# Start of a decode kernel: order of the first loads, longer rows for one weight, and two scalars over the software queue

## The chip, the cores and the metric

One core of one Trainium2 chip runs the kernel. Times are device microseconds. Before the change the kernel took 670.45 us (median of 3 runs, 669.8 to 670.9). The *span* is the part of an execution that the profile covers.

## The reference, cut to what matters

```python
x = A_x                                    # (4, 1, 640)
xn = layernorm(x)
# attention: q = xn @ wq (640 x 4096), 32 heads of 128; scores with k_cache (4,32,4096,128),
# softmax, times v_cache (4,32,4096,128), @ wo (4096 x 640)
# gMLP: z = gelu(xn @ w_in) (640 x 1728); z1, z2 = halves; z2 = layernorm(z2)
#       g = w_sp * z2 + b_sp               # w_sp and b_sp are one bf16 number each, as S = 1
#       (z1 * g) @ w_out (864 x 640)
return x + attention(xn) + gmlp(xn)
```

Each number of the caches (268 MB) and of the weights (14 MB) is used once, so some 282 MB have to come from HBM.

## The kernel before

Five buffers of 128 x 16,384 bf16 (4 MB each) take turns. The first holds w_in and w_out, the next two hold wq, then k and v units of 4 MB follow. All of this goes through the hardware queue of the SyncE engine (queue 1). The two scalars and x go through the hardware queue of ScalarE (queue 10); the trace shows them issued there in another order than written, the scalars at 0.74 and 1.31 us and x behind them at 1.96. In the views, xnT is the normalised and transposed x, QZ the tile in which q is laid out for the scores, and k0 the first unit of k. A packet record is the trace's entry for one piece of work of one DMA engine: start, duration and bytes.

```python
wg = kv_tile("w_gmlp")
w_in = wg[:, 0:n_in].rearrange("p (c f) -> p c f", c=DC)
nc.sync.dma_start(out=w_in, in_=B_w_in.rearrange("(p c) f -> p c f", c=DC))     # 17,280 B rows
nf = (FC - 1) * P                                                               # 768
nc.sync.dma_start(out=w_out[:, 0:FC - 1, :], in_=B_w_out[0:nf, :].rearrange("(c p) n -> p c n", p=P))
nc.sync.dma_start(out=w_out[:FL, FC - 1, :], in_=B_w_out[nf:Fh, :])             # 96 rows
... # wq in two loads, rows of 24,576 and 16,384 B
nc.scalar.dma_start(out=x_bf, in_=x_flat)
nc.scalar.dma_start(out=sb_bf[:, 0:1], in_=B_w_sp.rearrange("a b -> (a b)").to_broadcast((P, 1)))
nc.scalar.dma_start(out=sb_bf[:, 1:2], in_=B_b_sp.to_broadcast((P, 1)))
... # constants, layernorm of x, xnT
... # gMLP: 70 matmuls with w_in, gelu, layernorm, uT
... # q: 160 matmuls with wq, shuffles into q3
... # 14 matmuls uT x w_out into proj; then the loop over 32 k units and 32 v units
```

The broadcast of a scalar to 128 partitions is 128 pieces of two bytes.

Of the kernel before, what the change touches and what calls it, by code (L numbers as in the profile page):

```python
# [11 lines left out]
F32 = mybir.dt.float32  # L12
BF16 = mybir.dt.bfloat16
# [3 lines left out]
def kernel(  # L17
# [19 lines left out]
    nc = tc.nc  # L37
    P = 128
    B, Sq, D = A_x.shape
    _, H, Sk, Dh = A_k_cache.shape  # L40
    assert Sq == 1 and B == 4 and Dh == P and D % P == 0
    DC = D // P
# [10 lines left out]
    F2 = B_w_in.shape[1]  # L53
    Fh = F2 // 2
    FC = (Fh + P - 1) // P
    FL = Fh - (FC - 1) * P
    NOUT = A_wo.shape[1]
# [6 lines left out]
    const = ctx.enter_context(tc.tile_pool(name="const", bufs=1))  # L64
# [14 lines left out]
    def misc_ps(shape, dtype):  # L79
        misc_ctr[0] += 1  # L80
        return ps_m.tile(shape, dtype, tag="misc", name=f"misc{misc_ctr[0]}")
# [3 lines left out]
    def kv_tile(name):  # L85
        return kvpool.tile([P, KV], BF16, tag="kv", name=name)
# [3 lines left out]
    out_flat = out.rearrange("b s d -> (b s) d")  # L90


    wg = kv_tile("w_gmlp")
    n_in = DC * F2
    w_in = wg[:, 0:n_in].rearrange("p (c f) -> p c f", c=DC)
    nc.sync.dma_start(out=w_in, in_=B_w_in.rearrange("(p c) f -> p c f", c=DC))
    w_out = wg[:, n_in:n_in + FC * NOUT].rearrange("p (c n) -> p c n", c=FC)
    nf = (FC - 1) * P
    nc.sync.dma_start(out=w_out[:, 0:FC - 1, :], in_=B_w_out[0:nf, :].rearrange("(c p) n -> p c n", p=P))
    nc.sync.dma_start(out=w_out[:FL, FC - 1, :], in_=B_w_out[nf:Fh, :])  # L100

    wq_v = A_wq.rearrange("(p c) n -> p c n", c=DC)
    wq_t = []
    for i, (c0, c1) in enumerate(((0, 3), (3, DC))):
        wt = kv_tile(f"wq{i}")
        n = (c1 - c0) * H * Dh
# [4 lines left out]
    x_bf = wt[:B, KV // 2 + 7 * D:KV // 2 + 8 * D]  # L111
    nc.scalar.dma_start(out=x_bf, in_=x_flat)
    sb_bf = const.tile([P, 2], BF16)
    nc.scalar.dma_start(out=sb_bf[:, 0:1], in_=B_w_sp.rearrange("a b -> (a b)").to_broadcast((P, 1)))
    nc.scalar.dma_start(out=sb_bf[:, 1:2], in_=B_b_sp.to_broadcast((P, 1)))
    sb_f = const.tile([P, 2], F32)


    ident_bf = const.tile([P, P], BF16)
# [28 lines left out]
    xnT = const.tile([P, DC, B], BF16)  # L148
# [23 lines left out]
    for bb in range(2):  # L172
        nc.vector.tensor_copy(out=SelG[:, bb, :, :, 2 * bb:2 * bb + 2],
                              in_=I32[:].rearrange("p (b h c) -> p c h b", b=2, c=NCH))
# [12 lines left out]
    Pm = const.tile([P, 4, HG, 32], BF16)  # L187
    for hd in range(HG):
        nc.vector.tensor_copy(out=Pm[:, :, hd, :].rearrange("p (a w) j -> p a w j", w=2),
                              in_=ident_bf[:].rearrange("p (a j w) -> p a w j", a=2, w=2))  # L190
# [9 lines left out]
    proj = ps_j.tile([64, 512], F32)  # L200


    zT_ps = ps_g.tile([P, 2, FC, B], F32)
    for part in range(2):
        for fc in range(FC):
            n = P if fc < FC - 1 else FL
            f0 = part * Fh + fc * P
            for c in range(DC):
                nc.tensor.matmul(zT_ps[:n, part, fc, :], lhsT=w_in[:, c, f0:f0 + n],  # L209
                                 rhs=xnT[:, c, :], start=(c == 0), stop=(c == DC - 1))  # L210
    zT = const.tile([P, 2, FC, B], F32)
    nc.vector.memset(zT[:], 0.0)
# [1 line left out]
    nc.vector.memset(uT[:], 0.0)  # L214
    nc.scalar.activation(out=zT[:, :, 0:FC - 1, :], in_=zT_ps[:, :, 0:FC - 1, :], func=ACT.Gelu_apprx_tanh)
    nc.scalar.activation(out=zT[:FL, :, FC - 1, :], in_=zT_ps[:FL, :, FC - 1, :], func=ACT.Gelu_apprx_tanh)
    nc.vector.tensor_copy(out=sb_f[:], in_=sb_bf[:])
    z1 = zT[:, 0, :, :]
    z2 = zT[:, 1, :, :]
    st_in = const.tile([P, 2, FC, B], F32)  # L220
# [4 lines left out]
                     rhs=st_in[:].rearrange("p s c b -> p (s c b)"), start=True, stop=True)  # L225
# [17 lines left out]
    nc.vector.tensor_scalar(out=t1[:], in0=t1[:], scalar1=sb_f[:, 0:1], scalar2=sb_f[:, 1:2],  # L243
                            op0=ALU.mult, op1=ALU.add)
    nc.vector.tensor_tensor(out=uT[:, :, 0:B], in0=z1, in1=t1[:], op=ALU.mult)


    q_ps = misc_ps([P, H, B], F32)
    for h in range(H):
        for c in range(DC):  # L250
            nc.tensor.matmul(q_ps[:, h, :], lhsT=wq_t[c][:, h * Dh:(h + 1) * Dh], rhs=xnT[:, c, :],  # L251
                             start=(c == 0), stop=(c == DC - 1))
    q_bf = const.tile([P, H * B], BF16)
    nc.vector.tensor_copy(out=q_bf[:], in_=q_ps[:].rearrange("p h b -> p (h b)"))
    q3_ps = misc_ps([P, 4, H * B], F32)
    for kw in range(4):
        nc.tensor.matmul(q3_ps[:, kw, :], lhsT=Pm[:, kw, :, :].rearrange("p a j -> p (a j)"), rhs=q_bf[:],
                         start=True, stop=True)
    q3 = const.tile([P, 4, H * B], BF16)
    nc.vector.tensor_copy(out=q3[:], in_=q3_ps[:])  # L260


    for fc in range(FC):
        n = P if fc < FC - 1 else FL
        nb = B if fc else 32
        for hf in range(NH):
            nc.tensor.matmul(proj[32 * hf:32 * hf + nb, 0:NO2], lhsT=uT[:n, fc, 0:nb],
                             rhs=w_out[:n, fc, hf * NO2:(hf + 1) * NO2], start=(fc == 0), stop=False)
# [221 lines left out]
    for s in range(NS):  # L490
# [19 lines left out]
        if 0 <= v < NU - 1:  # L510
            emit_V(v, vc)
            g, b = divmod(v, B)
# [8 lines left out]
        elif v == NU - 1 and vc == 0:  # L521
# [8 lines left out]
            for t in range(T):  # L530
                a, c, e = t // 64, t // 16 % 4, t % 16
# [40 lines left out]
```

## Time and profile before

| | before |
|---|---|
| span of the profiled run | 669.1 us |
| share of the DMA engines' time used by queue 1 | 98.6% |
| rate in the middle 609 us | 431 GB/s |
| first transpose of the first k unit (k0) starts | 37.91 us |
| PE, DVE busy | 50%, 48% |

The first transpose of k0, as the trace has it (37.91 is its start, 3.20 us the wait for k before it):

```profile
37.91 8.89 DVE L318 STREAM_TRANSPOSE kT<-k 128x2048 f32<-128x2048 f32 x4 [3.20 <-DMA k<-in_A_k_cache_dram]
```

The page's slices show the DMA rate in 40 slices of 16.7 us. All but the first and the last lie between 418 and 441 GB/s. A kernel like this can gain only at the ends of the stream or in its bytes, and the change is made to the first 30 us.

To measure that stretch I use a sum that the document calls **stream lost**. It takes the packet records of a trace, spreads the bytes of each over its duration, sets the first packet of queue 1 at 1.75 us, adds the bytes moved from 1.5 to 32.5 us, and counts by how many microseconds they fall short of 431 GB/s. For the kernel before it is 3.57 us. The lines of stretches count a packet where it starts, so a short stretch can differ there from this sum by some tens of GB/s.

### The profile page before, as it was taken

What the parts mean: (1) busy time and instruction counts of PE and PEld (TensorE: products, weight loads), DVE (VectorE), ACT (ScalarE), POOL (GpSimd) and SP (SyncE); (2) the same over time, 40 slices, a digit from 0 to 9 for tenths busy, and PEclk for the clock granted to TensorE, in tenths of its full rate; (3) what the DMA queues carried; (4) which work ended last, traced back from release to release, by engine and by line L of the source; (5) the groups of instructions that cost most, each with busy time, mean ns of one, the idle gap of its engine ahead of it and who ended that gap; (6) DMA issues with size and microseconds to landing.
All of it is one profiled execution on the core that took longest, in us unless ns stands there. A gap on an engine that the chain in (4) does not pass through costs nothing.

```text
span 669.1 us, 6401 instructions
## 1 busy us (share of the span) xinstructions
PE 335.7 (50%) x2781; PEld 139.1 (21%) x2781; DVE 319.5 (48%) x253; ACT 60.4 (9%) x184; POOL 8.9 (1%) x40
## 2 busy tenths in 40 slices
PE   0647463546543664337555364454753366433745
PEld 0511121122111221113121031111311122111323
DVE  4279853465533455542555534346543355543300
ACT  0200210012000210003000030001200021000300
POOL 0010000000000000000000000000000000000000
PEclk9997777778777787676766677866767878567676
DMA  8999999999999999999999999999999999999995
GB/s 313 439 424 428 436 433 428 425 436 431 426 435 430 428 434 439 424 428 434 427 429 433 432 427 434 426 427 441 428 431 430 431 427 432 433 433 426 435 418 230
DMA packets 12900, 282.65 MB, mean 422 GB/s; under 512 B 1621, under 2 KB 3017, under 8 KB 4169
## 3 DMA queue, kind: packets, MB, share of 16 engines
q1 hardware_dynamic: 12568, 282.25, 98.6%
q8 instruction: 21, 0.34, 0.2%
q10 hardware_dynamic: 304, 0.01, 0.0%
q14 instruction: 7, 0.05, 0.0%
HBM read 282.25 MB, written 0.01 MB: 422 GB/s over the span
## 4 chain that ended last, share of the span: by engine, by line
DMA 56%; PE 15%; issue 13%; DVE 12%; ACT 3%; ACTq 0%; DVEq 0%
DMA k<-in_A_k_cache_dram 50%; DVE kT L318 8%; PE O L422 6%; DMA wo_last<-in_A_wo_dram 5%; PE S L336 3%; ACT p L364 3%; PE misc L439 2%; DMA sb_bf<-in_B_b_sp_dram 2%; PE x L377 1%; DVE m L343 1%; DVE om L442 1%; PE misc L251 1%; PE misc L347 1%; ACT O_sb L430 0%; PE zT_ps L209 0%
## 5 line engine op out<-in xcount | busy, mean ns | idle before, releaser
L318 DVE STREAM_TRANSPOSE kT<-k 128x2048 f32<-128x2048 f32 x128 | 284.6, 2280 | 215.0 <-DMA k<-in_A_k_cache_dram 212.4
L336 PE MATMUL S<-kT,QZ 128*32 128x512 bf16 x1024 | 203.7, 538 | 257.6 <-DVE kT L318 255.2
L336 PEld LDWEIGHTS <-QZ 128*32 128x32 bf16 x1024 | 57.3, 115 | 399.1 <-issue 386.7
L422 PE MATMUL O<-v,Zb 128*32 128x512 bf16 x992 | 93.1, 467 | 9.0 <-DMA v<-in_A_v_cache_dram 9.0
L422 PEld LDWEIGHTS <-Zb 128*32 128x32 bf16 x992 | 42.1, 112 | 41.0 <-issue 26.2
L364 ACT ACTIVATE p<-S,negmax 128x1024 bf16<-128x1024 f32 x16 | 17.7, 1109 | 272.0 <-DVE negmax L358 272.0
L430 ACT COPY O_sb<-O 128x512 f32<-128x512 f32 x16 | 9.4, 585 | 240.6 <-PE O L422 240.6
L388 ACT COPY Zb<-x 32x128 bf16<-32x128 bf16 x128 | 27.3, 255 | 10.2 <-PE x L377 9.5
L377 PE MATMUL x<-IdP,p 128*128 128x128 bf16 x128 | 16.1, 305 | 18.9 <-ACT p L364 18.6
L442 DVE SCALAR_TENSOR_TENSOR om<-misc,rinv,MkH 16x512 bf16<-16x512 f32 x7 | 5.2, 739 | 37.8 <-PE misc L439 37.8
L439 PE MATMUL misc<-O_sb,SelG 128*16 128x128 f32 x112 | 16.9, 289 | 2.0 <-DVE rinv L398 1.5
L377 PEld LDWEIGHTS <-p 128*128 128x128 bf16 x128 | 12.0, 138 | 22.6 <-ACT p L364 22.6
L275 POOL COPY QZ<-q 32x16 bf16<-32x16 bf16 x32 | 7.9, 246 | 455.4 <-PE S L336 420.9
L439 PEld LDWEIGHTS misc<-O_sb,SelG 128*16 128x16 f32 x112 | 10.1, 99 | 7.9 <-ACT O_sb L430 2.4
L474 DVE TENSOR_TENSOR oL<-misc,rinv 128x8 bf16<-128x8 f32 (+1 forms) x2 | 0.3, 168 | 22.6 <-PE misc L472 22.6
L343 DVE TENSOR_REDUCE m<-S 128x1 f32<-128x512 f32 x8 | 5.5, 691 | 10.2 <-PE S L336 10.2
L147 PE MATMUL misc<-ident_bf,wq 4*128 4x4 bf16 x5 | 0.4, 178 | 18.9 <-DVE wq L143 18.9
L368 DVE TENSOR_TENSOR rowsum<-rs 128x1 f32<-128x1 f32 x8 | 1.2, 155 | 17.0 <-ACT p L364 17.0
L347 PE MATMUL misc<-dg,ones_f 128*128 128x128 f32 x16 | 3.9, 324 | 9.0 <-DVE dg L345 9.0
L364 ACT ACT_TABLE_LOAD x1 | 1.3, 1283 | 54.8 <-DVE negmax L358 54.8
L460 PE MATMUL proj<-wo,oT 128*4 128x320 bf16 x56 | 5.0, 298 | 1.9 <-DVE oT L453 1.9
L251 PE MATMUL misc<-xnT,wq 128*128 128x4 bf16 x160 | 4.7, 166 | 1.1 <-issue 0.8
(93 smaller groups left out, 75.9 us busy)
## 6 DMA issues: line engine op xcount, KB each, us to landing
k<-in_A_k_cache_dram SPq DMA_DIRECT2D x32, 4096.0 KB, 43.3
v<-in_A_v_cache_dram SPq DMA_DIRECT2D x31, 4096.0 KB, 41.1
wo<-in_A_wo_dram SPq DMA_DIRECT2D x7, 640.0 KB, 44.6
wq<-in_A_wq_dram SPq DMA_DIRECT2D x1, 3072.0 KB, 19.5
w_gmlp<-in_B_w_in_dram SPq DMA_DIRECT2D x1, 2160.0 KB, 9.3
wq<-in_A_wq_dram SPq DMA_DIRECT2D x1, 2048.0 KB
v<-in_A_v_cache_dram SPq DMA_DIRECT2D x1, 2048.0 KB
v<-in_A_v_cache_dram SPq DMA_DIRECT2D x1, 1024.0 KB, 38.4
```

The lines of the kernel that those rows point to most:

```text
L251: nc.tensor.matmul(q_ps[:, h, :], lhsT=wq_t[c][:, h * Dh:(h + 1) * Dh], rhs=xnT[:, c, :], start=(c == 0), stop=(c == DC - 1))
L318: nc.vector.transpose(kT[:], kw[:, ch * n:(ch + 1) * n])
L336: nc.tensor.matmul(S_ps[32 * q:32 * q + 32, :, :], lhsT=qz[:, b, kw, w0:w0 + 32], rhs=kT[:, i, :, kw // 2, :, kw % 2], start=(b == 0 and c ...
L343: nc.vector.tensor_reduce(out=m1[:], in_=S_ps[:].rearrange("p k m -> p (k m)"), axis=AX.X, op=ALU.max)
L347: nc.tensor.matmul(mm[:], lhsT=ones_f[:], rhs=dg[:], start=True, stop=True)
L364: nc.scalar.activation(out=p_i[:], in_=S_ps[:, 8 * i:8 * i + 8, None, :].to_broadcast((P, 8, HG, M)), func=ACT.Exp, bias=negmax[:, 0:1], s ...
L377: nc.tensor.transpose(x[:, t, :], p_bf[t // 8][:, t % 8].rearrange("p h m -> p (h m)"), IdP[:])
L388: nc.scalar.copy(out=dst, in_=src[:, 2 * bb + b1])
L422: nc.tensor.matmul(O_ps[32 * q:32 * q + 32, :, :], lhsT=Zb[bb][:, w0:w0 + 32], rhs=vv[:, e // 16, e % 16, :, :], start=(b1 == 0 and e < 4) ...
L430: nc.scalar.copy(out=O_sb[:], in_=O_ps[:])
L439: nc.tensor.matmul(oh[:], lhsT=SelG[:, bb, c].rearrange("p h b -> p (h b)"), rhs=O_sb[:, c, :], start=(bb == 0 and c == 0), stop=(bb == 1 ...
L442: nc.vector.scalar_tensor_tensor(out=om[:], in0=oh[:, None, :].to_broadcast((G, HG, Dh)), scalar=state.pop(("rinv", g))[:, 0:1], in1=MkH[: ...
```

## The change

The intent: load wq first and compute q first, so that what the attention needs is there early; give w_out long rows; take the scalars out of the way of x and of the hardware queues.

```diff
+    nc.sync.dma_start(wq ...)            # both halves first, then x on nc.scalar
-    nc.scalar.dma_start(out=sb_bf[:, 0:1], in_=B_w_sp...to_broadcast((P, 1)))
-    nc.scalar.dma_start(out=sb_bf[:, 1:2], in_=B_b_sp.to_broadcast((P, 1)))
+    nc.gpsimd.dma_start(out=sb_bf[:, 0:1], in_=B_w_sp...to_broadcast((P, 1)))
+    nc.gpsimd.dma_start(out=sb_bf[:, 1:2], in_=B_b_sp.to_broadcast((P, 1)))
...  # w_in, w_out now after wq
-    ... in_=B_w_out[0:nf, :].rearrange("(c p) n -> p c n", p=P))     # 768 rows of 1,280 B
+    ... in_=B_w_out[0:nf, :].rearrange("(p c) n -> p c n", p=P))     # 128 rows of 7,680 B
...  # q, q3 moved ahead of the gMLP
-                nc.tensor.matmul(..., lhsT=w_in[:, c, f0:f0 + n], ...)
+                    w = w_in[:, c, f0:f0 + nf].rearrange("p (f a) -> p a f", a=FC - 1)[:, fc, :]
+                nc.tensor.matmul(..., lhsT=w, ...)                   # every sixth column
-    nc.vector.tensor_copy(out=sb_f[:], in_=sb_bf[:])
+    nc.gpsimd.tensor_copy(out=sb_f[:], in_=sb_bf[:])
```

More of the change, by code (lines that the diff above doesn't have):

```diff
@@ L90 @@
     out_flat = out.rearrange("b s d -> (b s) d")
-    wg = kv_tile("w_gmlp")
-    n_in = DC * F2
-    w_in = wg[:, 0:n_in].rearrange("p (c f) -> p c f", c=DC)
-    nc.sync.dma_start(out=w_in, in_=B_w_in.rearrange("(p c) f -> p c f", c=DC))
-    w_out = wg[:, n_in:n_in + FC * NOUT].rearrange("p (c n) -> p c n", c=FC)
-    nf = (FC - 1) * P
-    nc.sync.dma_start(out=w_out[:, 0:FC - 1, :], in_=B_w_out[0:nf, :].rearrange("(c p) n -> p c n", p=P))
-    nc.sync.dma_start(out=w_out[:FL, FC - 1, :], in_=B_w_out[nf:Fh, :])
     wq_v = A_wq.rearrange("(p c) n -> p c n", c=DC)
@@ L113 @@
     sb_bf = const.tile([P, 2], BF16)
-    nc.scalar.dma_start(out=sb_bf[:, 0:1], in_=B_w_sp.rearrange("a b -> (a b)").to_broadcast((P, 1)))
-    nc.scalar.dma_start(out=sb_bf[:, 1:2], in_=B_b_sp.to_broadcast((P, 1)))
+    nc.gpsimd.dma_start(out=sb_bf[:, 0:1], in_=B_w_sp.rearrange("a b -> (a b)").to_broadcast((P, 1)))
+    nc.gpsimd.dma_start(out=sb_bf[:, 1:2], in_=B_b_sp.to_broadcast((P, 1)))
     sb_f = const.tile([P, 2], F32)
+    wg = kv_tile("w_gmlp")
+    n_in = DC * F2
+    w_in = wg[:, 0:n_in].rearrange("p (c f) -> p c f", c=DC)
+    nc.sync.dma_start(out=w_in, in_=B_w_in.rearrange("(p c) f -> p c f", c=DC))
+    w_out = wg[:, n_in:n_in + FC * NOUT].rearrange("p (c n) -> p c n", c=FC)
+    nf = (FC - 1) * P
+    nc.sync.dma_start(out=w_out[:, 0:FC - 1, :], in_=B_w_out[0:nf, :].rearrange("(p c) n -> p c n", p=P))
+    nc.sync.dma_start(out=w_out[:FL, FC - 1, :], in_=B_w_out[nf:Fh, :])
     ident_bf = const.tile([P, P], BF16)
@@ L200 @@
     proj = ps_j.tile([64, 512], F32)
+    q_ps = misc_ps([P, H, B], F32)
+    for h in range(H):
+        for c in range(DC):
+            nc.tensor.matmul(q_ps[:, h, :], lhsT=wq_t[c][:, h * Dh:(h + 1) * Dh], rhs=xnT[:, c, :],
+                             start=(c == 0), stop=(c == DC - 1))
+    q_bf = const.tile([P, H * B], BF16)
+    nc.vector.tensor_copy(out=q_bf[:], in_=q_ps[:].rearrange("p h b -> p (h b)"))
+    q3_ps = misc_ps([P, 4, H * B], F32)
+    for kw in range(4):
+        nc.tensor.matmul(q3_ps[:, kw, :], lhsT=Pm[:, kw, :, :].rearrange("p a j -> p (a j)"), rhs=q_bf[:],
+                         start=True, stop=True)
+    q3 = const.tile([P, 4, H * B], BF16)
+    nc.vector.tensor_copy(out=q3[:], in_=q3_ps[:])
     zT_ps = ps_g.tile([P, 2, FC, B], F32)
@@ L206 @@
             n = P if fc < FC - 1 else FL
-            f0 = part * Fh + fc * P
+            f0 = part * Fh
             for c in range(DC):
-                nc.tensor.matmul(zT_ps[:n, part, fc, :], lhsT=w_in[:, c, f0:f0 + n],
+                if fc < FC - 1:
+                    w = w_in[:, c, f0:f0 + nf].rearrange("p (f a) -> p a f", a=FC - 1)[:, fc, :]
+                else:
+                    w = w_in[:, c, f0 + nf:f0 + Fh]
+                nc.tensor.matmul(zT_ps[:n, part, fc, :], lhsT=w,
                                  rhs=xnT[:, c, :], start=(c == 0), stop=(c == DC - 1))
@@ L245 @@
     nc.vector.tensor_tensor(out=uT[:, :, 0:B], in0=z1, in1=t1[:], op=ALU.mult)
-    q_ps = misc_ps([P, H, B], F32)
-    for h in range(H):
-        for c in range(DC):
-            nc.tensor.matmul(q_ps[:, h, :], lhsT=wq_t[c][:, h * Dh:(h + 1) * Dh], rhs=xnT[:, c, :],
-                             start=(c == 0), stop=(c == DC - 1))
-    q_bf = const.tile([P, H * B], BF16)
-    nc.vector.tensor_copy(out=q_bf[:], in_=q_ps[:].rearrange("p h b -> p (h b)"))
-    q3_ps = misc_ps([P, 4, H * B], F32)
-    for kw in range(4):
-        nc.tensor.matmul(q3_ps[:, kw, :], lhsT=Pm[:, kw, :, :].rearrange("p a j -> p (a j)"), rhs=q_bf[:],
-                         start=True, stop=True)
-    q3 = const.tile([P, 4, H * B], BF16)
-    nc.vector.tensor_copy(out=q3[:], in_=q3_ps[:])
     for fc in range(FC):
```

## The prediction

> **What bounds the kernel now.** I read the page's queue table and slices first, because 282 MB for one core is a lot of traffic for 670 us.
>
> ```profile
> q1 hardware_dynamic: 12568, 282.25, 98.6%
> GB/s 313 439 424 428 436 433 428 425 436 431 426 435 430 428 434 439 424 428 434 427 429 433 432 427 434 426 427 441 428 431 430 431 427 432 433 433 426 435 418 230
> ...
> L318 DVE STREAM_TRANSPOSE kT<-k 128x2048 f32<-128x2048 f32 x128 | 284.6, 2280 | 215.0 <-DMA k<-in_A_k_cache_dram 212.4
> ...
> k<-in_A_k_cache_dram SPq DMA_DIRECT2D x32, 4096.0 KB, 43.3
> w_gmlp<-in_B_w_out_dram SPq DMA_DIRECT2D x1, 960.0 KB, 12.8
> ```
>
> One queue keeps the 16 DMA engines 98.6% busy. PE is busy 50% of the span and DVE 48%, and DVE's largest idle time, 212.4 us, is waiting for k to land. A k load lands a median 43.3 us after its issue. One 4 MB unit takes 4.194 MB / 431 GB/s = 9.7 us, so a load is issued with some 3.5 other units still ahead of it. A wait of an engine for a buffer, or of the issuing queue for a semaphore, therefore costs nothing unless it exceeds about 30 us. The chain of waits agrees: its largest item is the k loads, 50%.
>
> So the time is start-up, plus bytes over the rate, plus what the stream loses at its two ends, plus a short tail. I then cut the stream by stretches (columns: stretch, length, busy time of PE, PEld, DVE, ACT and POOL with counts, clock, DMA share, GB/s; a packet counts in the stretch in which it starts, so short stretches are rough):
>
> ```profile
> 0.00:5.00 5.00, 0.00 (x0) 0.00 (x0) 3.01 (x9) 1.28 (x1) 1.08 (x8) 1.00 0.66 218
> 5.00:8.00 3.00, 0.00 (x0) 0.00 (x0) 0.00 (x0) 0.00 (x0) 0.00 (x0) 1.00 0.97 363
> 8.00:11.00 3.00, 0.00 (x0) 0.00 (x0) 0.00 (x0) 0.00 (x0) 0.00 (x0) 1.00 0.68 216
> 11.00:15.00 4.00, 0.00 (x0) 0.00 (x0) 3.16 (x21) 0.00 (x0) 0.00 (x0) 1.00 1.12 413
> ...
> 25.00:634.00 609.00, 312.95 (x2431) 124.06 (x2431) 306.68 (x202) 53.08 (x169) 7.86 (x32) 0.74 1.00 431
> 634.00:660.00 26.00, 14.65 (x172) 8.35 (x171) 1.25 (x4) 2.57 (x9) 0.00 (x0) 0.74 0.98 414
> 660.00:669.00 9.00, 4.37 (x107) 3.23 (x103) 0.65 (x2) 0.00 (x0) 0.00 (x0) 0.51 0.24 87
> ```
>
> The middle 609 us run at 431 GB/s with all engines busy, and the change touches nothing there. The losses are in the first 15 us. From 0 to 5 us there is 1.76 us before the first packet and then a ramp (the first 17,280 B packets take 1.1 to 1.7 us each, later ones 0.644). From 5 to 15 us, 363x3 + 216x3 + 413x4 = 3,389 KB move where 4,310 could, so 921/431 = 2.1 us are lost. This is where w_out (row by row) and the two scalars are on the engines. The total loss available to the change is about this 2.1 us.
>
> The same 15 us hold the compute that the change reorders. The chain of waits begins there with the scalars:
>
> ```profile
> 1.31 10.32 DMA sb_bf<-in_B_b_sp_dram
> 13.57 0.53 DVE Pm L189 x4
> 14.11 0.41 DVE wq L130
> ...
> 25.72 2.05 PE proj L267 x14
> 27.78 3.53 PE misc L251 x129
> 31.31 0.79 issue
> 32.10 0.88 PE misc L251 x28
> 32.98 33.90 DMA k<-in_A_k_cache_dram
> ```
>
> DVE sits 7.5 us in its program order before the cast of the two scalars, and the layernorm of x (from 14.1) is behind it. The last line looks as though q, by releasing the wq buffers, sets when a k load starts. But that load lands 33.9 us after its issue because it queues behind others, so an earlier release only lengthens its queueing.
>
> **What the Trainium skill says.** "DMA: Bandwidth & Descriptors", section "Why small descriptors are slow (HBM only)", gives a fixed overhead per packet and per descriptor. The trace agrees in direction: 32,768 B packets take a median 1.215 us (27.0 GB/s per engine), 1,280 B packets 0.055 us median and 0.059 mean (21.6), 5,120 B packets 0.199 (25.8), 8,192 B packets 0.313 (26.1). The same page, section "Issuing engines are not separate DMA queues", says that DMAs from any issuing engine run on the same 16 engines and interleave. The trace shows it: the scalars' 2 B packets on queue 10 lie between the w_in and w_out packets of queue 1. Hence moving the scalars to the software queue should not remove their 256 packets. "SBUF — State Buffer", section on the port swizzle, note on SBUF cachelines, says consecutive reads that leave a 16 B line pay a penalty. The new w_in weight loads step 12 B between columns; no trace of before has such a load, its packed ones take 104 ns.
>
> **The change part by part.**
>
> 1. Order of the big loads: wq (5.24 MB) before w_in, w_out (3.32 MB). The sum before k0 is equal, so k0's position in the stream does not move. Alone worth 0.
>
> 2. w_out in rows of 7.5 KB: 768 packets of 1,280 B become 128 of 7,680 B. Transfer: 768 x 0.059 / 16 = 2.83 us before; 128 x 0.295 (estimate, 7,680 B at 26.0 GB/s from the rows above) / 16 = 2.36 us after; saves 0.5 us. On top, between 8 and 9.5 us the engines are about half idle in the packet records, 0.7 us of stream, just where w_in runs out and w_out starts, and w_out's packets do not yet flow. I think that the many small rows are not made fast enough, right at the front of the queue. After the change there are a sixth of the rows and 22 us of loads ahead of them, so I count most of this 0.7 as saved: 0.6. The last 96 rows of w_out stay at 1,280 B, a sixth of the packets of before, so some loss stays. Sum: 1.1 us.
>
> 3. Scalars on the software queue, x alone on the other: the 256 packets stay (9 ns each, 0.13 us per engine), but they come early, beside 24 KB packets. From 6.3 to 8 us the engines deliver 310 to 350 GB/s while 2 B packets alternate with 17,280 B ones; if that alternation is the cause, 0.3 to 0.4 us. I cannot tell whether it moves or goes. I count 0.2.
>
> 4. DVE no longer waits for the scalars, and x need not follow them. The layernorm can start at about 4.5 us (estimate, x issued at 0.7) in place of 14.1, and xnT be ready near 10 in place of 19.5. Then wq lands at about 1.8 + 5.24/0.431 + 1.5 ramp = 15.5 plus 1 for the last engine, against 26 before; q (160 matmuls, 4.7 us busy), the shuffles (2 us) and the QZ fill (2.4) end near 26 in place of 37.1. The gMLP waits for w_gmlp, near 24 to 25, and takes the 8.2 us that it took from 19.56 to 27.77, ending near 33; k0 lands near 36. All of it beside the stream: 0 us of the end. The strided weight loads, 60 of them, would cost 60 x 0.3 = 18 us even if four times as slow (estimate), and that too hides in the 30 us of queued loads.
>
> 5. The tail from 660 us on keeps its instructions and its order.
>
> Sum: 0 + 1.1 + 0.2 + 0 + 0 = 1.3 us. 670.45 - 1.3 = 669.15, say 669.2.
>
> **The rivals.**
>
> A. Nothing gained. Each load runs in 16 shares and the end is set by the slowest engine: in the records the engines finish between 659.5 and 664.5. If the engines that end last lost least in the first 15 us, the gain is eaten. Against: between 8 and 9.5 us the loss was on nearly all engines. It gives 670.2 to 670.8.
>
> B. The gain is up to the whole 2.1 us, and 0.3 of the ramp also goes since x and the scalars are out of the way: 668.2. For: 2 B packets and 1,280 B rows are everywhere in that stretch. Against: both remain in part.
>
> C. A new wait. The software queue's descriptors are made by GpSimd ahead of the identity matrices, which the transposes of x and IdP need; or the strided weight loads hold PE while k0 arrives, so that S starts late. For: in the new program order PE does the gMLP's last matmuls before the first S. Against: k0's buffer is not needed for a new load before the 30 us of queue are used up. A late start of even 15 us gives 0; only well above 30 us would the stream starve. It makes 671 to 680, chance 2%.
>
> D. The earlier q lets the whole pipeline start earlier, by the 11 us by which QZ is ready sooner: 660. The chain of waits suggests it. Against: the first transpose waits for k0, which lands at 37.9 whatever q does, and bytes over rate allow no such gain.
>
> **Range and chances.** The three runs of before spread over 1.1 us. The gain is 0 to 2.4. So 669.2, with 668.0 to 670.5 in 8 of 10. Two per cent is 13.4 us, and only a starved stream (C) or a gain that the bytes do not allow (D) gets there: faster 0.005, same 0.985, slower 0.01.
>
> **What would show it.** Right: the first slice of 16.7 us rises from 313 to about 340 GB/s, while the middle stays at 431; no dip to half where w_out runs; q ends near 26 us, gMLP near 33; the first transpose of k0 starts 1 to 1.5 us earlier than 37.9, and so does wo_last's landing. Step 2 is wrong if a dip of the same depth appears elsewhere; step 3 if the scalars' packets slow wq0; step 4 if S of k0 starts later than 40.3 and the loads near 75 us show gaps. The whole is wrong if the middle stretch leaves 431 GB/s.

## The result, and the profile after

The changed kernel took 670.16 us (median of 4 runs, 669.91 to 670.24) against 670.33 for the kernel before in the same measurement. The ratio is 0.9997, with a 95% interval of 0.9979 to 1.0014. Ratios here are the mean time of one kernel's fast runs over the mean of the other's of the same rounds, so not quite the ratio of the medians quoted. The time is the same, and inside the predicted range. The gain of 1.3 us did not show. The interval alone does not exclude it (1.3 us would be a ratio of 0.9981); that of the repeat further down does (0.9990 to 1.0021), and so does the stream lost.

The page of the changed kernel, its slices and its queues:

```profile
GB/s 329 429 420 429 437 437 421 429 441 420 431 437 421 436 434 433 422 434 434 423 434 434 427 433 432 429 430 435 429 432 431 430 431 433 428 434 429 430 425 243
...
q1 hardware_dynamic: 11928, 282.25, 98.7%
...
q0 software_dynamic: 64, 0.00, 0.0%
q10 hardware_dynamic: 16, 0.01, 0.0%
```

The first slice rose from 313 to 329 GB/s and not to 340; the rest is as before. Queue 1 has 640 packets fewer, which is w_out's 768 rows turned into 128. The scalars' 256 packets have gone from queue 10, and a queue 0 has come with 64.

The stretches of the changed kernel (columns as in the prediction):

```profile
0.00:5.00 5.00, 0.00 (x0) 0.00 (x0) 3.80 (x10) 1.28 (x1) 2.53 (x10) 1.00 0.70 232
5.00:8.00 3.00, 0.00 (x0) 0.00 (x0) 2.94 (x12) 0.48 (x2) 0.00 (x0) 1.00 0.49 205
8.00:11.00 3.00, 0.35 (x5) 0.27 (x5) 2.22 (x17) 1.09 (x1) 0.00 (x0) 1.00 1.06 451
11.00:15.00 4.00, 0.24 (x3) 0.16 (x3) 0.00 (x0) 0.00 (x0) 0.18 (x1) 1.00 0.94 403
...
25.00:634.00 609.00, 308.08 (x2316) 122.86 (x2315) 306.94 (x208) 55.97 (x178) 7.12 (x29) 0.74 1.00 430
634.00:660.00 26.00, 14.49 (x191) 8.39 (x190) 1.25 (x4) 1.57 (x4) 0.00 (x0) 0.72 0.98 414
```

The weak stretch from 8 to 11 us has gone (216 to 451 GB/s), and the stretch from 5 to 8 us has fallen from 363 to 205, with the engines busy for half of it. In the packet records the rate between 6.0 and 8.0 us is 240, 56, 68 and 106 GB/s in its half microseconds. This hole costs 1.6 us of stream. It lies in the first wq load, whose packets are of 24,576 B, and the first records of queue 0 follow at 6.6 us.

The compute of the start behaved about as predicted. From the changed kernel's order of time:

```profile
9.61 0.35 PE L148 MATMUL misc<-ident_bf,wq 4*128 4x4 bf16 x5 [9.61 <-DVE wq L144]
...
17.91 4.34 PE L207 MATMUL misc<-xnT,wq 128*128 128x4 bf16 x157 [4.66 <-DMA wq<-in_A_wq_dram]
...
24.02 2.42 POOL L280 COPY QZ<-q 32x16 bf16<-32x16 bf16 x8 [11.65 <-DVE q L216]
...
30.55 2.05 PE L272 MATMUL proj<-w_gmlp,uT 128*32 128x320 bf16 x14 [2.30 <-DVE uT L265]
...
36.59 8.89 DVE L323 STREAM_TRANSPOSE kT<-k 128x2048 f32<-128x2048 f32 x4 [6.10 <-DMA k<-in_A_k_cache_dram]
```

The columns are start, time from start to end, engine, line, operation, and in brackets the idle time before and what ended it. The transposes of x start at 9.6 us instead of 18.9, QZ is full at 26.4 instead of 37.1, the gMLP ends at 32.6, and the first transpose of k0 waits 6.1 us for its load. All of this is early, and the time shows none of it.

That first transpose starts 1.3 us earlier than before, and the span is 0.9 us shorter. So two of the prediction's signs of being right, an earlier k0 and an earlier wo_last (its matmuls start at 663.89 instead of 664.95), did appear. But that profiled pair flatters the change. In the 9 timed runs of the kernel before in the first batch below, the spans alternate between 667.9 to 668.0 and 668.8 to 669.1, and its profile is one of the long ones. The first four spans of the changed kernel are 667.9 to 668.2. Why the spans have two levels is open. Other kernels show the upper one too, and k0's first transpose can carry it: e5 below was profiled at 668.9 us and has it at 37.39, with no more stream lost than the changed kernel (36.59). By stream lost the pair differs by 0.16 us (3.57 and 3.41), which is nearer to what the clock says.

### The profile page after: what moved, and what is told of

It reads as the page before. It is cut to its first block, busy times and chain, and to the rows that moved or that the text cites. A ratio compares the mean times of both kernels' runs of the same rounds, so it can differ in the third digit from the quotient of the medians.

```text
span 668.2 us, 6403 instructions
## 1 busy us (share of the span) xinstructions
PE 333.3 (50%) x2781; PEld 140.6 (21%) x2781; DVE 318.8 (48%) x252; ACT 60.4 (9%) x184; POOL 10.6 (2%) x43
## 4 chain that ended last, share of the span: by engine, by line
DMA 66%; PE 12%; issue 11%; DVE 9%; ACT 2%; SPq 0%; DVEq 0%; ACTq 0%
DMA k<-in_A_k_cache_dram 52%; DMA v<-in_A_v_cache_dram 7%; DVE kT L323 6%; PE O L427 5%; DMA wo_last<-in_A_wo_dram 5%; PE S L341 3%; DMA wq<-in_A_wq_dram 2%; ACT p L369 2%; PE x L382 1%; PE misc L444 1%; PE misc L207 1%; DVE m L348 1%; PE misc L352 0%; DVE om L447 0%; ACT O_sb L435 0%
## 5 line engine op out<-in xcount | busy, mean ns | idle before, releaser
L341 PE MATMUL S<-kT,QZ 128*32 128x512 bf16 x1024 | 200.8, 532 | 261.3 <-DVE kT L323 258.9
L427 PE MATMUL O<-v,Zb 128*32 128x512 bf16 x992 | 91.1, 463 | 8.9 <-DMA v<-in_A_v_cache_dram 8.9
L382 PE MATMUL x<-IdP,p 128*128 128x128 bf16 x128 | 16.1, 305 | 18.9 <-ACT p L369 18.6
L207 PEld LDWEIGHTS <-wq 128*128 128x128 bf16 x160 | 4.4, 104 | 7.9 <-DMA wq<-in_A_wq_dram 7.9
## 6 DMA issues: line engine op xcount, KB each, us to landing
wq<-in_A_wq_dram SPq DMA_DIRECT2D x1, 3072.0 KB, 12.2
```

Of the source, the lines that this page charges most:

```text
L207: nc.tensor.matmul(q_ps[:, h, :], lhsT=wq_t[c][:, h * Dh:(h + 1) * Dh], rhs=xnT[:, c, :], start=(c == 0), stop=(c == DC - 1))
L341: nc.tensor.matmul(S_ps[32 * q:32 * q + 32, :, :], lhsT=qz[:, b, kw, w0:w0 + 32], rhs=kT[:, i, :, kw // 2, :, kw % 2], start=(b == 0 and c ...
L382: nc.tensor.transpose(x[:, t, :], p_bf[t // 8][:, t % 8].rearrange("p h m -> p (h m)"), IdP[:])
L427: nc.tensor.matmul(O_ps[32 * q:32 * q + 32, :, :], lhsT=Zb[bb][:, w0:w0 + 32], rhs=vv[:, e // 16, e % 16, :, :], start=(b1 == 0 and e < 4) ...
```

## The experiments

Stated theory: the hole is the scalars' doing, and it gave back what the rows of w_out had gained (theory S). Rival: a hole belongs to the start of the stream, whatever the scalars do (H). Every kernel was compared with the kernel before in the same rounds. The expectations place the hole at 5 to 7.5 us; I had set the zero of the packet records 0.7 us off, and in span time it is 6 to 8 us. All outputs passed the check; e2 and e4 do not compute what the reference asks, and pass because w_sp is near 0 and b_sp near 1. e1, e2, e5 and e3 ran on another chip than the later runs, so a time of one group says less beside a time of the other.

| run | edit | median us | ratio to before (95%) | stream lost, us |
|---|---|---|---|---|
| before | | 670.39 to 670.61 in three batches | | 3.57 |
| changed | | 670.16 | 0.9997 (0.9979 to 1.0014) | 3.41 |
| e1_scalars_hw | changed, scalars on ScalarE's queue | 669.53 | 0.9990 (0.9978 to 1.0003) | 2.83 |
| e2_no_scalars | changed, scalars not loaded | 668.31 | 0.9974 (0.9960 to 0.9987) | 1.79 |
| e5_scalars_late | changed, scalars issued at 11.5 us | 670.10 | 1.0003 (0.9991 to 1.0016) | 3.39 |
| e3_wout_short | changed, w_out in short rows | 670.66 | 1.0009 (0.9997 to 1.0022) | 3.93 |
| e6_one_row_hw | changed, one piece per scalar, ScalarE's queue | 668.06 | 0.9968 (0.9954 to 0.9981) | 1.70 |
| e9_one_row_sw | changed, one piece per scalar, software queue | 668.55 | 0.9973 (0.9959 to 0.9986) | 1.76 |
| e4_before_no_scalars | before, scalars not loaded | 668.58 | 0.9974 (0.9960 to 0.9987) | 2.31 |
| e8_order_only | before, new order alone | 670.08 | 0.9996 (0.9982 to 1.0009) | 3.50 |
| e11_after_again | changed, unedited | 670.36 | 1.0005 (0.9990 to 1.0021) | 3.47 |
| e10_scalars_twice | changed, scalars loaded twice | 672.15 | 1.0025 (1.0011 to 1.0039) | 4.16 |
| e12_scalars_twice_hw | e1 with scalars loaded twice | 670.30 | 1.0000 (0.9986 to 1.0014) | 3.18 |
| e7_wout_96 | e6 with w_out as 96 long rows | 670.72 | 1.0007 (0.9994 to 1.0019) | 3.86 |

The intervals of e2, e6, e9, e4 (faster) and e10 (slower) exclude 1; all differences are below 2%.

### The scalars back on the hardware queue

```diff
-    nc.gpsimd.dma_start(out=sb_bf[:, 0:1], ...)   # and [:, 1:2]
+    nc.scalar.dma_start(out=sb_bf[:, 0:1], ...)   # and [:, 1:2]
```

> The changed kernel, with only the two scalars back on the hardware queue of the scalar engine. In its own profile the changed kernel has a hole: from 5.0 to 7.5 us the 16 engines moved about a third of what they could (by the packet records 1.6 us of stream lost). Theory S (the software queue's scalar packets make the hole): the hole goes; instead the 256 two-byte packets cost 0.3 to 0.6 us spread over the first 10 us; the first transpose of k0 starts 0.8 to 1.3 us earlier than 36.6. Rival H (the hole belongs to the start of the hardware queue, whatever the scalars do, since the kernel before has one too, from 8 to 9.5 us): a hole of 1 us or more is still there in the first 10 us and k0's first transpose stays at 36.2 to 37. Time: S gives 669.0 to 669.6 if before is 670.3, H 670.0 to 670.4.

Measured: 669.53 us. Its five runs (669.33 to 669.72) lie below all runs of the changed kernel. Two stretches of this run:

```profile
5.00:8.00 3.00, 0.00 (x0) 0.00 (x0) 0.00 (x0) 0.00 (x0) 0.00 (x0) 1.00 0.93 393
8.00:11.00 3.00, 0.00 (x0) 0.00 (x0) 0.00 (x0) 0.00 (x0) 0.00 (x0) 1.00 0.95 341
```

The hole to half has gone (393 instead of 205 GB/s), and a weaker, longer loss has come, 1.0 us in all against the run without scalars (2.83 - 1.79). S is right about the hole but put the loss on the hardware queue at 0.3 to 0.6 us, so k0's first transpose gained 0.7 us (35.92) and not 0.8 to 1.3. In this order x is behind the first scalar and the layernorm starts late again; the end does not notice.

### No scalars

```diff
-    nc.gpsimd.dma_start(out=sb_bf[:, 0:1], ...)
-    nc.gpsimd.dma_start(out=sb_bf[:, 1:2], ...)
+    nc.gpsimd.memset(sb_bf[:, 0:1], 0.0)
+    nc.gpsimd.memset(sb_bf[:, 1:2], 1.0)
```

> The changed kernel with the two scalars not loaded at all but set to 0 and 1 on GpSimd (not what the reference asks for, although the outputs will hardly differ since w_sp is near 0 and b_sp near 1). Theory S (the scalars' packets make the hole): no hole; from the third microsecond to 22 us the stream runs at 420 to 432 GB/s; k0's first transpose starts at 34.8 to 35.4 and the span shrinks by 1.3 to 1.6 us against the changed kernel. Rival H: the hole between 5 and 7.5 us stays, k0's first transpose at 36.2 to 37, span within 0.4 us of the changed kernel.

Measured: 668.31 us, k0's first transpose at 34.89, span 666.4, which is 1.8 us less than the changed kernel's 668.2 and a little more than the 1.3 to 1.6 expected.

```profile
5.00:8.00 3.00, 0.00 (x0) 0.00 (x0) 2.97 (x10) 0.15 (x1) 0.00 (x0) 1.00 0.99 426
```

In the packet records no half microsecond from 5 us to 20 us is below 427 GB/s, and nothing beyond the ramp (1.2 us) is lost to 20 us. The hole is the scalars'. H falls.

### The scalars later

```diff
+    nc.gpsimd.tensor_copy(out=sb_bf[:], in_=xnT[:, 0, 0:2])   # makes the loads wait for xnT
     nc.gpsimd.dma_start(out=sb_bf[:, 0:1], ...)               # moved behind xnT; and [:, 1:2]
```

> The changed kernel with its two software-queue loads held back until the normalised x is there (about 10 us instead of 1.2 us). Theory S: no hole at 5 to 7.5 us, and a hole of the same size, 1.3 to 1.8 us of stream, some 4 us after the new issue, between 13 and 17 us; k0's first transpose stays at 36.2 to 37. Rival H: the hole stays at 5 to 7.5 us. Third way: the hole comes only from software packets meeting the start of a stream; then it goes and nothing takes its place, k0's first transpose near 35.

Measured: 670.10 us (three runs at 670.0 to 670.1, two at 670.8 and 671.1). Issued at 11.5 and 12.2 us, the loads make their hole from 15.5 to 18.5 us, 1.5 us deep:

```profile
5.00:8.00 3.00, 0.00 (x0) 0.00 (x0) 2.95 (x11) 0.35 (x2) 0.00 (x0) 1.00 0.95 410
...
15.00:20.00 5.00, 2.55 (x95) 2.56 (x96) 0.00 (x0) 0.00 (x0) 0.00 (x0) 1.00 0.79 301
```

The stretch from 5 to 8 us is back at 410 GB/s, and the one from 15 to 20 us falls to 301 (430 in the changed kernel). So the hole follows the issue by 4 to 5 us and does not depend on the start of the stream. It needs no counted instruction of VectorE or GpSimd beside it either: the line shows none from 15 to 20 us. It ended about 1.5 us later than I had put it. k0's first transpose, at 37.39, is 0.4 us later than expected; the profile is of one of the two long runs.

### w_out back in short rows

```diff
-    ... B_w_out[0:nf, :].rearrange("(p c) n -> p c n", p=P)
+    ... B_w_out[0:nf, :].rearrange("(c p) n -> p c n", p=P)       # and w_in read packed
```

> The changed kernel with w_out back in rows of 1,280 B (and w_in read packed), the order and the software queue as changed. By the step of the prediction, the short rows cost 0.5 us of transfer; the other 0.6 us came from their being made too slowly at the front of the queue, and behind 22 us of loads they should not. Theory R (short rows cost only their transfer when they are deep in the queue): the hole at 5 to 7.5 us is as in the changed kernel, the stretch of w_out takes 0.4 to 0.8 us longer, k0's first transpose at 37.0 to 37.5, span 0.4 to 0.8 us above the changed kernel. Rival (they also starve the engines there): the stretch has a dip below 200 GB/s and costs 1 us or more.

Measured: 670.66 us, 3.93 us lost against 3.41 and 3.47: the long rows are worth 0.5 us of stream. All five runs (670.52 to 671.31) lie above the first four of the changed kernel (669.91 to 670.24), though its repeat reaches among them (670.19 to 671.36). The profile is of the longest run, and k0's first transpose is at 37.40, inside the expected range. Where w_out runs, the rate falls to between 290 and 370 GB/s and never near 200. This agrees with the theory of transfer alone: behind 20 us of loads short rows starve nothing.

### One piece per scalar

```diff
-    sb_bf = const.tile([P, 2], BF16)
-    nc.gpsimd.dma_start(out=sb_bf[:, 0:1], in_=B_w_sp...to_broadcast((P, 1)))
-    nc.gpsimd.dma_start(out=sb_bf[:, 1:2], in_=B_b_sp.to_broadcast((P, 1)))
+    sb_bf = const.tile([1, 2], BF16)
+    nc.scalar.dma_start(out=sb_bf[:, 0:1], in_=B_w_sp)            # e9: nc.gpsimd
+    nc.scalar.dma_start(out=sb_bf[:, 1:2], in_=B_b_sp[None, :])   # e9: nc.gpsimd
+    one_r = const.tile([1, P], BF16)
+    nc.vector.memset(one_r[:], 1.0)
 ...
-    nc.gpsimd.tensor_copy(out=sb_f[:], in_=sb_bf[:])
+    sb_ps = misc_ps([P, 2], F32)
+    nc.tensor.matmul(sb_ps[:], lhsT=one_r[:], rhs=sb_bf[:], start=True, stop=True)
+    nc.vector.tensor_copy(out=sb_f[:], in_=sb_ps[:])
```

> The changed kernel with each scalar loaded as one 2-byte packet into one partition over the scalar engine's hardware queue, and spread to 128 partitions by a matmul with a row of ones: a right kernel with 2 scalar packets in place of 256. The run without scalars lost only 1.2 us of stream by the 20th microsecond and measured 668.3. Theory S (it is the number of scalar packets): the same here, no hole and no slow stretch before w_out, k0's first transpose at 34.7 to 35.3, 668.1 to 668.8. Rival (any transfer beside the big ones at the start costs, through its queue and not its packets): 0.4 us or more stays, k0's first transpose at 35.3 to 36, 669.0 to 669.7.

Measured: 668.06 us (667.98 to 668.42), ratio 0.9968, the fastest kernel and a right one. Its stretches and its first transpose:

```profile
5.00:8.00 3.00, 0.00 (x0) 0.00 (x0) 0.20 (x1) 0.00 (x0) 0.00 (x0) 1.00 0.99 428
8.00:11.00 3.00, 0.00 (x0) 0.00 (x0) 2.93 (x9) 0.00 (x0) 0.00 (x0) 1.00 1.00 429
...
20.00:26.00 6.00, 4.83 (x95) 4.52 (x92) 1.15 (x3) 0.00 (x0) 2.03 (x8) 1.00 1.08 423
```

```profile
34.72 2.31 DVE L327 STREAM_TRANSPOSE kT<-k 128x2048 f32<-128x2048 f32 x1 [5.10 <-DMA k<-in_A_k_cache_dram]
```

The stream runs at full rate from the end of its ramp to w_out, and k0 is there 1.9 us before the changed kernel's. The expectation of theory S holds, but for a time 0.04 us below its range. The matmul that spreads the two numbers takes 0.16 us, beside the loads.

The same with the software queue:

> The same one-packet scalars, but over the software queue. It tells whether the 1.6 us hole comes with the first use of the software queue or with the many small packets. Queue theory: a hole of 1 us or more between 4 and 9 us stays, k0's first transpose at 36.0 to 36.8. Packet theory: the hole shrinks with the packets to under 0.3 us, k0's first transpose at 34.7 to 35.3, span as with one packet over the hardware queue within 0.4 us.

Measured: 668.55 us, 1.76 us lost, k0's first transpose at 34.76. The software queue has 64 records here, as in the changed kernel; but two of 2 B and 62 of 4 B take the place of 32 of 16 B and 32 of 4 B, and 5 to 8 us run at 410 GB/s (429 with the bytes spread over the packets' durations):

```profile
5.00:8.00 3.00, 0.00 (x0) 0.00 (x0) 2.97 (x10) 0.04 (x1) 0.00 (x0) 1.00 0.96 410
```

So neither the queue nor the number of its records makes the hole. What went is the 256 two-byte pieces; I take one 16 B record to hold eight of them (32 x 8 = 256). With them went the broadcast, 128 reads of one address. No run separates small pieces from repeated reads of one address.

### The kernel before without scalars

```diff
-    nc.scalar.dma_start(out=sb_bf[:, 0:1], ...)
-    nc.scalar.dma_start(out=sb_bf[:, 1:2], ...)
+    nc.vector.memset(sb_bf[:, 0:1], 0.0)
+    nc.vector.memset(sb_bf[:, 1:2], 1.0)
```

> The kernel before with the scalars set on VectorE and not loaded (not what the reference asks for, though the outputs will hardly differ). By the packet records the kernel before lost 3.5 us of stream to 20 us, 1.2 of it the ramp. The prediction blamed the half-idle stretch at 8 to 9.5 us on w_out's many short rows. If that holds, the stretch stays, and 2.5 to 3.3 us are lost to 20 us; time 669.7 to 670.4. If the scalars make it (the run of the changed kernel with its scalars on the hardware queue still lost 1.2 us on them), the stretch goes, 1.8 to 2.4 us are lost, and the time is 668.7 to 669.5.

Measured: 668.58 us, 2.31 us lost to 32.5 us, 2.22 of it to 20 us. The half-idle stretch has gone:

```profile
8.00:11.00 3.00, 0.00 (x0) 0.00 (x0) 2.54 (x5) 0.78 (x2) 0.00 (x0) 1.00 1.20 405
11.00:15.00 4.00, 2.90 (x75) 2.83 (x75) 0.62 (x4) 1.27 (x4) 0.00 (x0) 1.00 0.98 392
```

From 8 to 11 us it moves 405 GB/s where the kernel before moves 216 (371 and 256 with the bytes spread over the packets' durations; in the half-idle part from 8 to 9.5 us, 397 and 180). So that stretch was not made by w_out's short rows, as the prediction had it, but by the scalars. What the short rows cost is the rest, down to 280 to 310 GB/s for 1.5 us from 10.5 us on. Taking away the scalars from the kernel before brings 1.8 us; the whole change brought 0.2, which is within the noise. The time was a little below what I had expected of this theory.

### The order alone

```diff
     (the changed kernel)
-    ... long w_out rows, w_in every sixth column, scalars on nc.gpsimd
+    ... short w_out rows, w_in packed, scalars on nc.scalar
```

> The kernel before with the new order alone: wq first and q before the gMLP, w_out in short rows, the scalars over the scalar engine's hardware queue (the first one ahead of x, the second behind it). By the prediction the order is worth 0: 670.0 to 670.9, stream lost to 32 us 3.2 to 3.7 us as before. If the half-idle stretch needs short scalars and short rows at the same time, the order does gain, since w_out then comes at 21 us when the scalars are long done: lost 3.0 or less, 669.4 to 670.0.

Measured: 670.08 us, 3.50 us lost. That is 0.07 us of stream from the kernel before and a ratio of 0.9996. The order is worth nothing that can be measured, as predicted (the cast of the scalars stays on GpSimd here, as in the changed kernel).

```profile
8.00:11.00 3.00, 0.00 (x0) 0.00 (x0) 0.00 (x0) 0.00 (x0) 0.00 (x0) 1.00 0.75 270
```

The weak stretch stays with the scalars at 8 to 11 us (336 GB/s with the bytes spread), although wq's long rows run there now and w_out comes only at 21 us. It is shallower than before; the rows of w_out lose their part later.

### The changed kernel again, and the scalars twice

> The changed kernel once more, unedited, beside the others of this batch and with an interval of its own. Its first measurement was 670.16. Every theory: 669.9 to 670.3, 2.8 to 3.0 us of stream lost to 20 us, k0's first transpose at 36.4 to 36.9.

Measured: 670.36 us (670.19 to 670.49, and one at 671.36); 3.47 us lost to 32.5 us, 2.73 of it by 20 us, slightly less than expected.

```diff
     nc.gpsimd.dma_start(out=sb_bf[:, 0:1], ...)   # and [:, 1:2]
+    sb_2 = const.tile([P, 2], BF16)
+    nc.gpsimd.dma_start(out=sb_2[:, 0:1], ...)    # and [:, 1:2]; e12: both pairs on nc.scalar
```

> The changed kernel with both scalars loaded a second time, into a tile that nobody reads, over the same software queue: 512 two-byte pieces in place of 256. Without scalars the stream lost 1.8 us to 32 us, with 256 pieces 3.4. Piece theory (each two-byte piece holds its engine for some 0.1 us whatever its record of 15 ns for eight of them says; 16 pieces per engine make 1.6 us): another 1.4 to 1.8 us is lost, 4.8 to 5.2 us to 32 us, time 671.4 to 672.0. Rival (a fixed cost of small pieces on the software queue, however many): 3.2 to 3.6 us and 670.0 to 670.4.

Measured: 672.15 us, 4.16 us lost. Twice the pieces cost 1.8 us more time (672.15 against 670.36), a little more than the piece theory said; but only 0.7 us more of stream to 32.5 us, half of what it said and well above what the rival allows. The first 256 pieces made the same hole as before (2.65 us lost by 10 us; the changed kernel 2.85 and 2.73), and the second 256 a shallower one. So on the software queue a second set costs again, and not in proportion in the first 32 us. The other part of the 1.8 us comes later: the last data land 1.6 us after those of the repeated changed kernel. Why the later part is lost is open.

> The same doubling with the scalars on the scalar engine's hardware queue, where 256 pieces cost 1.1 us of stream (2.8 lost to 32 us against 1.7). Piece theory: some 0.07 us per piece there, so another 0.9 to 1.3 us, 3.7 to 4.2 us lost to 32 us, time 670.4 to 671.0. Rival (the hardware queue's cost is one of starting up beside the big loads): 2.7 to 3.0 and 669.4 to 669.8.

Measured: 670.30 us, 0.8 us above e1, and 3.18 us lost, 0.35 more than e1. Both numbers miss the piece theory's range at its low end and lie outside the rival's. e1 ran in another batch, and half of the 0.35 us lies before 12.5 us, where both kernels run the same 128 pieces, so that a second set costs on this queue is not shown. "So many nanoseconds for a piece" is no constant: the first 256 cost 1.7 us of stream on the software queue (3.41 - 1.70) and 1.1 us on the hardware queue (2.83 - 1.70). Divided by 16 pieces per engine that would be an estimate of 0.11 and 0.07 us for each, though their records last 9 ns for one or 15 ns for eight.

The packet records of e1 show that this average hides something. The first scalar's 128 pieces run from 5.1 to 12.5 us, and from 5 to 12.5 us 1.18 us of stream are lost. Then come x and the second scalar's 128 pieces, to 18.1 us, and from 12.5 to 20 us only 0.05 us are lost. e8 shows the same (1.41 and 0.05), and in e12 171 pieces run from 12.5 to 20 us for 0.06. On the software queue, too, the loss comes at the start: 1.53 us from 6.0 to 8.5 us with 15 of the 32 records of 16 B, and 0.04 from 8.5 to 12 us with the other 17 (1.36 and 0.18 in the repeat). So half of the pieces ran at almost no cost. What makes the first ones dear is open.

### w_out as 96 long rows

```diff
     (the kernel with one piece per scalar)
-    nc.sync.dma_start(out=w_out[:, 0:FC - 1, :], in_=B_w_out[0:nf, :].rearrange("(p c) n -> p c n", p=P))
-    nc.sync.dma_start(out=w_out[:FL, FC - 1, :], in_=B_w_out[nf:Fh, :])
+    nc.sync.dma_start(out=w_out[:96], in_=B_w_out.rearrange("(p c) n -> p c n", p=96))   # 9 rows of n each
 ...  # 9 chunks of 96 columns of w_in, every ninth one
```

> The kernel with one packet per scalar on the hardware queue (668.06), with w_out loaded in one transfer as 96 rows of 11.5 KB, so that the last 96 rows of 1,280 B go too. In that kernel 0.5 us of stream are lost between 20 and 26 us, where w_out runs. Theory (short rows lose it): 0.1 to 0.3 us are lost there, time 667.7 to 668.1. Rival (96 partitions share out worse over the 16 engines than 128, or the change from 17 KB rows to k loses it): 0.5 us or more stays lost, 668.0 to 668.6.

Measured: 670.72 us, 2.7 us slower than without the edit. The expectation's theory falls, and its rival is far too small. Two lines, the stretch of w_out and the weight loads of the gMLP (count, busy us, mean ns):

```profile
20.00:26.00 6.00, 4.84 (x52) 4.52 (x50) 1.14 (x3) 0.00 (x0) 1.98 (x8) 1.00 1.02 253
```

```profile
L225 PEld LDWEIGHTS <-w_gmlp 128*96 128x96 bf16 x90 | 15.6, 267 | 0.8 <-DMA w_gmlp<-in_B_w_in_dram 0.8
```

The stream falls from 423 to 253 GB/s over these six microseconds (395 to 253 with the bytes spread), with the engines busy all the time. The 96 packets of 11,520 B take a median of 0.766 us, which is 15 GB/s per engine; the 7,680 B packets of the 128-partition load take 0.291 us, 26 GB/s. Stream lost grows by 2.2 us, most of the 2.7. So this transfer into 96 partitions ran at little over half the rate of the one into 128. Its rows are longer as well, but the 17,280 B rows of w_in take 0.644 us, 27 GB/s per engine, so length is not the likely reason. Beside such loads the first 32 KB packets of k are slow as well (1.9 to 2.2 us instead of 1.22), and in the kernel with one piece per scalar the first of them take 1.5 to 1.6 us beside the last 96 short rows. So part of the 0.5 us that is still lost there may come from 96 partitions and not from short rows; no run separates the two, nor tells why 96 partitions are slow. The second line is the gMLP's matmuls at 267 ns per weight load: it ends at 44 us and holds up DVE and PE, but with queued loads behind it. Whether this adds to the 0.5 us that the stream does not explain is open.

## Why the prediction was right or wrong

The time fell in the range, 1 us above its middle. That is owed to the width of the range, in which the unchanged kernel's 670.33 lies too: the sum did not come out, and two of its terms fail. The signs that the prediction had named for this both came: a dip appeared elsewhere (step 2), and the scalars' packets slowed wq (step 3).

1. **Order, 0 us.** Right: 3.57 to 3.50 us of stream with the order alone, ratio 0.9996.

2. **w_out, 1.1 us.** The mechanism "longer rows take less transfer" was right, and its term of 0.5 us was about right: 0.67 us from e8 to e1 (3.50 - 2.83), 0.52 us from e3 to the changed kernel (3.93 - 3.41). The failed step is the other 0.6 us, "the many small rows are not made fast enough, right at the front of the queue". Without the scalars that dip was not there (405 instead of 216 GB/s from 8 to 11 us), with the short rows left at the front. (A slip beside it: the last 96 rows are a ninth of the 864 rows of before, not a sixth of their packets.) I read the cause off what lay at the same time; both suspects lay there.

3. **Scalars, a gain of 0.2 us.** Wrong in sign. That the pieces stay and still run on the same 16 engines was right. But I took their records of 9 ns for their cost. With them 1.1 us of stream go on the hardware queue and 1.7 on the software queue. So the change lost 0.6 us here (3.41 - 2.83; by the medians 670.16 against 669.53).

4. **Earlier compute, 0 us.** Right: its ends came within about half a microsecond of their estimates (QZ 26.4 for "near 26", gMLP 32.6 for "near 33"), and the end of the kernel did not follow. On the way there some were further off: the layernorm began at 2.8 instead of 4.5 us, the bulk of q waited for wq until 17.9 instead of 16.5, and the gMLP began at 23.1 instead of 24 to 25 and took 9.5 us instead of 8.2. S of k0 started at 38.95, before the 40.3 that would have been the sign of a fault. In e1 the layernorm is as late as before, and that kernel is faster than the changed one. The strided weight loads took 144 ns instead of 105, far from four times.

5. **Tail, 0 us.** Its order and its work are the same, and no run was made for it.

In stream, term by term: 0.07 + 0.67 - 0.58 = 0.16 us, where I had 1.3. The steps come from single profiles with a scatter of about 0.06 us in the one kernel run twice (3.41, 3.47). The clock agrees in order: 670.4, 670.08, 669.53, 670.16.

Of the rivals, none is what happened. A's "nothing gained" comes within 0.04 us of the right number (670.2 to 670.8), for another reason: there was hardly a gain for the slowest engine to eat (0.16 us of stream). C, a new wait, did not come. D, the hope in an earlier q, is refuted by the result itself: QZ was full 10.7 us earlier and the time stayed. B's figure of 668.2 is what could be had, and e6 gets it (668.06) by the part that the change left in: no longer 256 pieces.

What stays open: why the stream loses so much when the two-byte pieces come, while half of them pass at no cost; whether their size or their common address does it; why it is worse on the software queue; and why a second set there costs less of the early stream. Also open is where the time outside the span comes from: 1.7 to 1.8 us in most runs of the kernel before, 2.0 in those of the changed kernel, 2.3 with the scalars twice on the software queue; e1 has about 2.0 without that queue. That 0.2 us is as large as the measured difference of the change.

## What to carry to other kernels

When a stream of large loads bounds a kernel, look for small pieces in it before moving or reordering anything, and distrust their records: a broadcast of one number to 128 partitions by DMA is 128 pieces, and loading each scalar once and spreading it with a matmul brought 2.1 to 2.3 us here (668.06 against the changed kernel's 670.16 and 670.36). A dip in the stream belongs to everything that is in flight during it, so take each suspect away alone before crediting one. Long rows are not enough: check that a transfer fills all 128 partitions, since the one into 96 ran at 15 GB/s per engine instead of 26.

## What the Trainium skill lacked or had wrong

- "DMA: Bandwidth & Descriptors", section "Why small descriptors are slow (HBM only)", gives a few cycles per packet. The runs show 1.1 us of stream lost with 256 two-byte pieces on the hardware queue, nearly all of it while the first 128 run, where 16 records of 9 ns on each engine add up to 0.14 us. The page names a least size for full rate, but has no figure for what pieces as small as these cost a stream of large packets.
- The same page, section "Issuing engines are not separate DMA queues": the engines are shared, as it says. It lacks what such pieces cost by queue: 1.7 us over the software queue against 1.1 us over the hardware queue.
- The same page, section "Why a DMA increments its semaphore by 16 and not by 1", gives a 96-partition tile all 16 engines, as many as 128 partitions have. The page's rules do ask for 128 partitions, but no page has a measured rate for 96: the run with 11,520 B packets into 96 partitions moved 15 GB/s per engine against 26 into 128.
- Nothing to mend in "SBUF — State Buffer", note on cachelines, which the prediction used; the trace agrees with its direction: 128-column weight loads went from 105 ns packed to 144 ns with a step of 12 B; 96-column ones from 187 ns packed to 267 ns with 18 B.
